# A pair's hash bits in one PSUM bank, their rows moved by DMA, and loads and transposes rearranged over the queues of a one-core attention and FFN kernel

## The chip, the cores and the metric

One core of one Trainium2 chip. The metric is device time in microseconds (us). Unless it says otherwise, a time is the median of a kernel's runs, and a line from a profile is from one profiled run of that kernel. A run is marked slow when it lies over 1.5% above the fastest of the same kernel; comparisons use the fast ones. Engine names: PE is TensorE's matmul, PEld its weight load, DVE VectorE, ACT ScalarE, POOL GpSimd, SP SyncE, whose queue here carries DMAs only. Two times belong to a DMA: its issue, in which the engine of its queue is held to hand it out, and its landing, from then until the data are there. The granted clock is the share of its full clock that TensorE was given (1.00 is full). In a line of a profile, `qT<-hb` reads "tile qT written from tile hb", and L205 is line 205 of that kernel.

## The reference, cut to what matters

```python
# q, k, v: (4 batches, 8 heads, 768 tokens, 64); proj: (64, 6)
q_bits = einsum('bhsd,dk->bhsk', q, proj) > 0          # six hash bits a token
k_bits = einsum('bhsd,dk->bhsk', k, proj) > 0
mask   = q_bucket[:, :, :, None] == k_bucket[:, :, None, :]
scores = where(mask, q @ k.T / 8, -1e9)
attn   = softmax(scores) @ v                           # then heads side by side: x is (3072, 512)
h      = maximum(maximum(x @ w1, x @ w2), x @ w3)      # three times 512 -> 768
out    = h @ w_out                                     # 768 -> 512
```

## The kernel before

Heads are worked in pairs, four pairs a batch. q and k are split into an fp16 high part and an fp16 residual, transposed, and multiplied by the two halves of `proj` (PA and PB, 32 columns each, so four groups lie side by side in a PSUM bank). The sign of each bit, scaled, becomes rows 64 to 69 of the transposed q and k. The scores then contract over 70 rows, and a pair in different buckets gets so low a score that its exponential is zero. So the first score of a pair waits for: load, splits, transpose, hash matmuls, compare, rows.

The program is a list of 192 steps, 48 a batch. A step is one score unit (two matmuls and one exponential) and whatever preparation the schedule puts there with `at(step, fn)`; FFN matmuls ("atoms") fill in as a credit allows. They share three PSUM buffers with the transposes and hash matmuls.

```python
def xbar(n, b, pr):                       # transpose by DMA, on SP's queue
    nc.sync.dma_start_transpose(T[n, b, pr][:], S16[n, b, pr][:].rearrange("p a d -> p (a d)"))

def hash_half(b, pr, half):               # one PSUM bank and one compare for each half of the tokens
    ...
    hps = hash_mm([(tq, 0, half), (tk, 0, half), (tq, 1, half), (tk, 1, half)])
    hash_cmp(hbs[b, pr][:, half * HQ : (half + 1) * HQ], hps)

def hash_rows(b, pr, heads=(0, 1)):       # DVE copies 6 partitions at a time, scaling them
    ...
        dst = T[n, b, pr][D : D + NBITS, hh * NCH : (hh + 1) * NCH, :].rearrange("p a t -> p (a t)")
        hash_row(dst, hb[32 * g : 32 * g + NBITS, :])

def prep(b, pr, s, lead, lag):            # pairs of batches 1 to 3
    at(s - lead, lambda: load_pair(b, pr, nc.gpsimd))
    ...
        at(s + 2 * i, lambda n=n: split_h(n, b, pr, nc.vector))
        at(s + 2 * i + 1, lambda n=n: split_r(n, b, pr))
        at(s + 2 * i + 1, lambda n=n: xbar(n, b, pr))
    tail(b, pr, s + lag)                  # hash_half, hash_half, hash_rows, hash_rows, one a step
```

Within a step the order is: score, attend, the scheduled functions, FFN atoms.

The softmax here doesn't subtract the row's maximum and nothing guards it: scores larger than these inputs give would overflow.

## Time and profile before

| | before |
|---|---|
| median of 3 runs | 340.19 us (340.01, 340.19, 345.54; the last a slow one) |
| span of the profiled run | 336.0 us |
| first score | 11.2 us |
| first score to first FFN matmul (stage A) | 54.8 us |
| first FFN matmul to last score (stage B) | 246 us |
| last score to the end (stage C) | 24.0 us |

The three stages have different limits, so they are read apart: in A there is no FFN work yet to fill PE with, in B PE should never stand, C is the last FFN half behind the last score. The lines are in the prediction below. One is added here, stage B as a whole (columns: stretch, length, busy time of PE, PEld, DVE, ACT and POOL, then the clock granted to PE, the DMA share, GB/s):

```profile
66.00:312.00 246.00, 220.75 (x2163) 135.94 (x2160) 153.01 (x299) 151.88 (x200) 42.85 (x53) 0.94 0.56 101
```

PE is idle for 25 of these 246 us and runs at 0.94 of its clock. The lines that matter here of what it waited for in the whole run (engine, tile and line, what it waited for; total us, times, longest):

```profile
PE tps L161 <- DVE qs L151: 6.9, 2, 5.0
PE ps L311 <- DVE ht L318: 5.2, 4, 3.1
PE hps L176 <- DMA kT<-ks: 4.6, 3, 3.4
PE xps L297 <- DVE ht L318: 4.2, 2, 2.8
...
PE hps L176 <- DMA qT<-qs: 3.3, 1, 3.3
```

The first is mostly the start, before the first score (5.0 us). For the rest, PE waits for DVE's max (`ht`, which frees a PSUM buffer), 12.7 us with the smaller lines, and the hash matmuls wait for DMA transposes.

### The profile page before, as it was taken

What the parts mean: (1) busy time and instruction counts of PE and PEld (TensorE: products, weight loads), DVE (VectorE), ACT (ScalarE), POOL (GpSimd) and SP (SyncE); (2) the same over time, 40 slices, a digit from 0 to 9 for tenths busy, and PEclk for the clock granted to TensorE, in tenths of its full rate; (3) what the DMA queues carried; (4) which work ended last, traced back from release to release, by engine and by line L of the source; (5) the groups of instructions that cost most, each with busy time, mean ns of one, the idle gap of its engine ahead of it and who ended that gap; (6) DMA issues with size and microseconds to landing.
All of it is one profiled execution on the core that took longest, in us unless ns stands there. A gap on an engine that the chain in (4) does not pass through costs nothing.

```text
span 336.0 us, 6898 instructions
## 1 busy us (share of the span) xinstructions
PE 288.1 (86%) x2800; PEld 177.3 (53%) x2800; DVE 212.6 (63%) x424; ACT 195.0 (58%) x254; POOL 67.8 (20%) x89
## 2 busy tenths in 40 slices
PE   1798696966998969799698987969989999999795
PEld 1465474542565546366365654636655666665352
DVE  3688969652998585937549585593775544453452
ACT  2467657651766647377275762746756776777120
POOL 1225625441041130403104040040200000000000
PEclk9999878595999999989699995997999999999899
DMA  7909989999969693590903927069442001001002
GB/s 228 334 3 142 208 168 237 161 181 106 200 93 155 142 162 76 106 221 13 210 16 107 223 59 177 22 139 124 53 91 97 2 0 64 33 0 64 32 2 94
DMA packets 52481, 38.20 MB, mean 114 GB/s; under 512 B 39009, under 2 KB 46497, under 8 KB 52449
## 3 DMA queue, kind: packets, MB, share of 16 engines
q1 hardware_dynamic: 44240, 20.26, 33.7%
q0 software_dynamic: 7984, 17.30, 23.7%
q8 instruction: 22, 0.36, 0.4%
q10 hardware_dynamic: 224, 0.20, 0.3%
q14 instruction: 11, 0.08, 0.1%
HBM read 25.17 MB, written 6.29 MB: 94 GB/s over the span
## 4 chain that ended last, share of the span: by engine, by line
PE 56%; DVE 24%; DMA 15%; issue 3%; ACT 1%; ACTq 0%; SPq 0%; DVEq 0%
PE ps L311 23%; PE sc L246 13%; DMA kT<-ks 13%; PE av L266 7%; PE po L323 6%; DVE qs L151 4%; DVE kT L185 3%; DVE ks L145 3%; DVE qT L185 3%; PE hps L176 3%; DVE ks L151 3%; DVE hb L181 2%; DVE ht L318 2%; PE tps L161 2%; DMA k<-in_k_dram 1%
## 5 line engine op out<-in xcount | busy, mean ns | idle before, releaser
L250 ACT ACTIVATE AT<-sc,bias_t 128x768 f16<-128x768 f32 x192 | 170.4, 903 | 97.8 <-PE sc L246 96.9
L311 PE MATMUL ps<-xT,w_sb 128*128 128x384 f16 x576 | 118.6, 342 | 8.7 <-DVE ht L318 5.2
L246 PE MATMUL sc<-qT,kT 70*128 70x384 f16 x384 | 102.2, 349 | 2.2 <-DVE qT L185 1.2
L318 DVE TENSOR_TENSOR ht<-ht,ps 128x384 f16<-128x384 f16 x96 | 52.9, 551 | 52.0 <-PE ps L311 49.3
L266 PEld LDWEIGHTS <-AT 128*128 128x128 f16 x1152 | 64.4, 101 | 33.7 <-issue 10.5
L311 PEld LDWEIGHTS <-w_sb 128*128 128x128 f16 x576 | 53.1, 101 | 42.4 <-issue 18.1
L266 PE MATMUL av<-vone,AT 128*128 128x65 f16 x1152 | 70.2, 198 | 3.4 <-DVE t L282 2.7
L287 POOL TENSOR_TENSOR xn<-t,rr 128x384 f16<-128x384 f32 x24 | 20.9, 870 | 224.4 <-DVE rr L285 134.7
L246 PEld LDWEIGHTS <-kT 70*128 70x128 f16 x384 | 34.6, 103 | 26.0 <-issue 10.0
L316 ACT CAST ht<-ps 128x384 f16<-128x384 f32 x48 | 22.8, 476 | 25.2 <-PE ps L311 25.1
L323 PE MATMUL po<-wout_sb,ht 128*128 128x512 f16 x144 | 35.0, 380 | 2.6 <-DVE ht L318 2.5
L181 DVE TENSOR_SCALAR hb<-hps 128x384 f16<-128x384 f32 x32 | 17.4, 545 | 22.9 <-PE hps L176 22.9
L282 DVE TENSOR_TENSOR t<-av,mv 128x390 f32<-128x390 f32 x32 | 17.9, 560 | 10.9 <-PE av L266 10.8
L323 PEld LDWEIGHTS <-ht 128*128 128x128 f16 x144 | 12.9, 97 | 16.3 <-DVE ht L318 3.0
L151 DVE SCALAR_TENSOR_TENSOR qs<-q,qs 128x768 f16<-128x768 f32 (+1 forms) x17 | 19.4, 1142 | 2.0 <-ACT qs L143 1.7
L329 DVE COPY osb<-po 128x512 f32<-128x512 f32 x16 | 11.0, 690 | 12.1 <-PE po L323 12.0
L217 POOL CAST vone<-v 128x768 f16<-128x768 f32 x16 | 15.1, 941 | 14.8 <-DMA v<-in_v_dram 14.8
L151 DVE SCALAR_TENSOR_TENSOR ks<-k,ks 128x768 f16<-128x768 f32 (+1 forms) x17 | 15.9, 936 | 2.3 <-ACT ks L143 1.9
L297 PE MATMUL xps<-iden,xn 128*128 128x128 f16 x96 | 11.5, 233 | 6.8 <-DVE ht L318 4.2
L176 PE MATMUL hps<-kT,PA 128*32 128x384 f16 x64 | 12.6, 366 | 5.4 <-DMA kT<-ks 4.6
L298 DVE COPY xT<-xps 128x384 f16<-128x384 f16 x32 | 11.3, 352 | 8.3 <-PE xps L297 7.8
L176 PE MATMUL hps<-qT,PA 128*32 128x384 f16 x64 | 13.0, 365 | 4.1 <-DMA qT<-qs 3.3
(46 smaller groups left out, 190.8 us busy)
## 6 DMA issues: line engine op xcount, KB each, us to landing
out_dram<-osb SPq DMA_DIRECT2D x24, 256.0 KB, 2.3
q<-in_q_dram POOLq DMA_DIRECT2D x12, 384.0 KB, 3.8
k<-in_k_dram POOLq DMA_DIRECT2D x12, 384.0 KB, 5.9
v<-in_v_dram POOLq DMA_DIRECT2D x12, 384.0 KB, 9.5
w_sb<-in_moe_w_dram POOLq DMA_DIRECT2D x6, 384.0 KB, 6.1
v<-in_v_dram SPq DMA_DIRECT2D x4, 384.0 KB, 6.5
q<-in_q_dram SPq DMA_DIRECT2D x3, 384.0 KB, 6.3
k<-in_k_dram SPq DMA_DIRECT2D x3, 384.0 KB, 6.8
```

The source lines that it names most:

```text
L151: nc.vector.scalar_tensor_tensor(out=s[:, a, D : 2 * D], in0=x32, scalar=QS, in1=s[:, a, 0:D], op0=AluOp.mult, op1=AluOp.subtract)
L176: nc.tensor.matmul(hps[32 * g : 32 * (g + 1), 0:HQ], w[:], t[:, a : a + CH, :], start=s, stop=not s)
L181: nc.vector.tensor_scalar(out=out, in0=hps[:, 0:HQ], scalar1=0.0, scalar2=0.5, op0=AluOp.is_gt, op1=AluOp.subtract)
L185: nc.vector.tensor_scalar(out=dst, in0=src, scalar1=2 * BIT, scalar2=None, op0=AluOp.mult)
L246: nc.tensor.matmul(sc[:, i, 0:HQ], kT[0:KR, hh * NCH + 2 * j + i, :], qT[0:KR, hh * NCH + hf * CH : hh * NCH + (hf + 1) * CH, :], start=Tr ...
L250: nc.scalar.activation(AT[:], sc[:, :, 0:HQ], ActFn.Exp, bias=bias_t[:], scale=EXP_SCALE)
L266: nc.tensor.matmul(av[:, o : o + D + 1], AT[:, i, c * P : (c + 1) * P], vones[b % 2][:, 2 * pr + hh, 2 * j + i, 0 : D + 1], start=first, s ...
L287: eng.tensor_tensor(out=xv, in0=t[:, :, :, 0:D], in1=rr[:].to_broadcast([P, 2, CH, D]), op=AluOp.mult)
L311: nc.tensor.matmul(ps[:, 0:HQ], w_sb[i][:, jc, fb * P : (fb + 1) * P], xT[:, jc, :], start=jc == 0, stop=jc == NJ - 1)
L316: nc.scalar.copy(ht[:], ps[:, 0:HQ])
L318: nc.vector.tensor_tensor(out=hts[fb][:], in0=hts[fb][:], in1=ps[:, 0:HQ], op=AluOp.max)
L323: nc.tensor.matmul(ps[:], hts[fb][:, c * P : (c + 1) * P], wout_sb[:, fb, :], start=fb == 0, stop=fb == NF - 1)
```

## The change

The intent: take work from DVE (the hash rows, half of the compares, the scaling half of the k splits), keep what is left of it out of the FFN's way, take batch 1's transposes from the DMA engines to PE, and keep Pool for the weights and for casting V.

```diff
-    raw = ... bufs=3        spl = ... bufs=2
+    raw = ... bufs=4        spl = ... bufs=3
-    load("k", 0, 0, nc.scalar, (0, 1))
+    load("k", 0, 0, nc.sync, (0, 1))
...
+    def hash_pair(b, pr):                       # both halves accumulate in one bank, 12 of 32 rows used
+        hb = small.tile([P, HQ], FP16, tag="hb", name="hb")
+        g = [(T[n, b, pr], hh) for hh in range(2) for n in "qk"]
+        hash_cmp(hb[:], hash_mm([[(t, hh, half) for t, hh in g] for half in range(2)]))
+        hash_row(hb[:], hb[:])                  # one scaling of the whole tile
+
+    def hash_rows(b, pr):                       # eight DMAs of 6 partitions x 768 bytes
+        ...
+                nc.sync.dma_start(T[n, b, pr][D : D + NBITS, a : a + CH, :].rearrange("p a t -> p (a t)"),
+                                  hb[o : o + NBITS, :])
...
     def front(b, pr, s):                        # TensorE transposes: batch 0, and now batch 1 too
+        at_end(s, lambda: split_h("q", b, pr, nc.vector))
+        at_end(s, lambda: split_h("k", b, pr, nc.vector if b == 0 else nc.scalar))
+        at_end(s, lambda: split_r("q", b, pr))
+        at_end(s + 1, lambda: split_r("k", b, pr))
...
     def prep(b, pr, s):                         # batches 2 and 3
+        at_end(s, lambda: split_h("q", b, pr, nc.vector))
+        at_end(s + 1, lambda: split_h("k", b, pr, nc.scalar))
+        at_end(s + 1, lambda: split_r("q", b, pr))
+        at_end(s + 1, lambda: xbar("q", b, pr))
+        at_end(s + 3, lambda: split_r("k", b, pr))
+        at_end(s + 3, lambda: xbar("k", b, pr))
+        tail(b, pr, s + 12)                     # hash_pair and hash_rows in one step
...
-                prep(b, pr, 26 + 7 * pr, 7, 12)
-                prep(b, pr, 2 * (b - 1) * NUG + 6 + 12 * pr, 10, 12)
+            s = 33 + 7 * pr if b == 1 else 2 * (b - 1) * NUG + 4 + 11 * pr
+            at(s - 8, lambda b=b, pr=pr: load_pair(b, pr, nc.sync))
+            (front if b == 1 else prep)(b, pr, s)
...
         if late:
             attend(u - LAG)
+        for fn in todo_end.pop(u, []):          # at_end: behind the step's FFN atoms
+            fn()
```

Cut: two sets of PA and PB (one for each half of the tokens), the copy of the first kT out of PSUM by DVE instead of ACT, PA and PB made behind the first splits, and smaller moves of the weight loads.

More of the change, by code (lines that the diff above doesn't have):

```diff
@@ L50 @@
     konst = ctx.enter_context(tc.tile_pool(name="konst", bufs=1))
-    raw = ctx.enter_context(tc.tile_pool(name="raw", bufs=3))
-    spl = ctx.enter_context(tc.tile_pool(name="spl", bufs=2))
+    raw = ctx.enter_context(tc.tile_pool(name="raw", bufs=4))
+    spl = ctx.enter_context(tc.tile_pool(name="spl", bufs=3))
     opnd = ctx.enter_context(tc.tile_pool(name="opnd", bufs=8))
@@ L104, with make_p @@
     ph = konst.tile([D, NBITS], FP16, name="ph")
-    PA = konst.tile([P, 32], FP16, name="PA")
-    PB = konst.tile([P, 32], FP16, name="PB")
-    nc.vector.memset(PA[:], 0.0)
-    nc.vector.memset(PB[:], 0.0)
     pr32 = konst.tile([D, NBITS], FP32, name="pr32")
-    def make_p():
-        nc.vector.tensor_copy(ph[:], p32[:])
-        nc.vector.tensor_tensor(out=pr32[:], in0=p32[:], in1=ph[:], op=AluOp.subtract)
+    PA, PB = [], []
+    for i in range(2):
+        for n, l in (("PA", PA), ("PB", PB)):
+            l.append(konst.tile([P, 32], FP16, name=f"{n}{i}", tag=f"{n}{i}"))
+            nc.vector.memset(l[i][:], 0.0)
+    def make_p(i):
+        if i == 0:
+            nc.vector.tensor_copy(ph[:], p32[:])
+            nc.vector.tensor_tensor(out=pr32[:], in0=p32[:], in1=ph[:], op=AluOp.subtract)
         for o in (0, D):
-            nc.vector.tensor_scalar(out=PA[o : o + D, 0:NBITS], in0=ph[:], scalar1=1024.0, scalar2=None,
-                                    op0=AluOp.mult)
-            nc.vector.tensor_scalar(out=PB[o : o + D, 0:NBITS], in0=pr32[:], scalar1=1024.0, scalar2=None,
-                                    op0=AluOp.mult)
+            for l, src in ((PA, ph), (PB, pr32)):
+                nc.vector.tensor_scalar(out=l[i][o : o + D, NBITS * i : NBITS * (i + 1)], in0=src[:],
+                                        scalar1=1024.0, scalar2=None, op0=AluOp.mult)
     w_sb = [konst.tile([P, NJ, DF], FP16, name=f"w{i}_sb") for i in range(3)]
@@ L169, in evac_T, with hash_mm @@
             nc.vector.tensor_copy(o, p16[:, c0 * P : c1 * P])
-    def hash_mm(groups):
+    def hash_mm(sets):
         hps = mm_ps.tile([P, 512], FP32, tag="mm", name="hps")
-        for s, w in ((True, PA), (False, PB)):
-            for g, (t, hh, half) in enumerate(groups):
+        ws = [(i, l[i]) for l in (PA, PB) for i in range(len(sets))]
+        for m, (i, w) in enumerate(ws):
+            for g, (t, hh, half) in enumerate(sets[i]):
                 a = hh * NCH + half * CH
                 nc.tensor.matmul(hps[32 * g : 32 * (g + 1), 0:HQ], w[:], t[:, a : a + CH, :],
-                                 start=s, stop=not s)
+                                 start=m == 0, stop=m == len(ws) - 1)
         return hps
@@ L187 @@
     hbs = {}
-    def hash_half(b, pr, half):
-        if half == 0:
-            hbs[b, pr] = small.tile([P, S], FP16, tag="hb", name="hb")
-        tq, tk = T["q", b, pr], T["k", b, pr]
-        hps = hash_mm([(tq, 0, half), (tk, 0, half), (tq, 1, half), (tk, 1, half)])
-        hash_cmp(hbs[b, pr][:, half * HQ : (half + 1) * HQ], hps)
-    def hash_rows(b, pr, heads=(0, 1)):
-        hb = hbs[b, pr]
-        for g, (n, hh) in enumerate((("q", 0), ("k", 0), ("q", 1), ("k", 1))):
-            if hh not in heads:
-                continue
-            dst = T[n, b, pr][D : D + NBITS, hh * NCH : (hh + 1) * NCH, :].rearrange("p a t -> p (a t)")
-            hash_row(dst, hb[32 * g : 32 * g + NBITS, :])
+    def hash_pair(b, pr):
+        hb = small.tile([P, HQ], FP16, tag="hb", name="hb")
+        hbs[b, pr] = hb
+        g = [(T[n, b, pr], hh) for hh in range(2) for n in "qk"]
+        hash_cmp(hb[:], hash_mm([[(t, hh, half) for t, hh in g] for half in range(2)]))
+        hash_row(hb[:], hb[:])
+    def hash_rows(b, pr):
+        hb = hbs.pop((b, pr))
+        for g, (n, hh) in enumerate((("q", 0), ("k", 0), ("q", 1), ("k", 1))):
+            for half in range(2):
+                a = hh * NCH + half * CH
+                o = 32 * g + NBITS * half
+                nc.sync.dma_start(T[n, b, pr][D : D + NBITS, a : a + CH, :].rearrange("p a t -> p (a t)"),
+                                  hb[o : o + NBITS, :])
     def hash_head(b, pr, hh):
         tq, tk = T["q", b, pr], T["k", b, pr]
-        hb = small.tile([P, S], FP16, tag="hb", name="hb")
-        hps = hash_mm([(tk, hh, 0), (tq, hh, 0), (tk, hh, 1), (tq, hh, 1)])
-        hash_cmp(hb[:, 0:HQ], hps)
+        hb = small.tile([P, HQ], FP16, tag="hb", name="hb")
+        hash_cmp(hb[:], hash_mm([[(tk, hh, 0), (tq, hh, 0), (tk, hh, 1), (tq, hh, 1)]]))
         for g, (t, half) in enumerate(((tk, 0), (tq, 0), (tk, 1), (tq, 1))):
@@ L212, in hash_head @@
             hash_row(t[D : D + NBITS, a : a + CH, :].rearrange("p a t -> p (a t)"),
-                     hb[32 * g : 32 * g + NBITS, 0:HQ])
+                     hb[32 * g : 32 * g + NBITS, :])
     def vcast(b, pr):
@@ L343, with at_end @@
     todo = {}
+    todo_end = {}
     def at(step, fn, pe=0.0):
         todo.setdefault(step, []).append((pe, fn))
+    def at_end(step, fn):
+        todo_end.setdefault(step, []).append(fn)
     operands(0, 0)
@@ L351 @@
     split_h("k", 0, 0, nc.scalar, (0, 1))
-    make_p()
     split_r("q", 0, 0, (0, 1))
     split_r("k", 0, 0, (0, 1))
+    make_p(0)
     pq = pe_T("q", 0, 0, 0)
@@ L357 @@
     evac_T(pq, "q", 0, 0, 0, nc.vector)
-    evac_T(pk, "k", 0, 0, 0, nc.scalar)
+    evac_T(pk, "k", 0, 0, 0, nc.vector)
     split_h("q", 0, 0, nc.scalar, (1, 2))
@@ L362 @@
     hash_head(0, 0, 0)
+    make_p(1)
     vcast(0, 0)
@@ L381, in front @@
         at(s, lambda: operands(b, pr))
-        at(s, lambda: split_h("q", b, pr, nc.vector))
-        at(s, lambda: split_r("q", b, pr))
-        at(s + 1, lambda: split_h("k", b, pr, nc.vector))
-        at(s + 1, lambda: split_r("k", b, pr))
+        at_end(s, lambda: split_h("q", b, pr, nc.vector))
+        at_end(s, lambda: split_h("k", b, pr, nc.vector if b == 0 else nc.scalar))
+        at_end(s, lambda: split_r("q", b, pr))
+        at_end(s + 1, lambda: split_r("k", b, pr))
         def tr(n, hh):
             evac_T(pe_T(n, b, pr, hh), n, b, pr, hh, nc.vector)
-        for i, (n, hh) in enumerate((("q", 0), ("k", 0), ("q", 1), ("k", 1))):
-            at(s + 3 + i // 2, lambda n=n, hh=hh: tr(n, hh), 0.34)
-        tail(b, pr, s + 5)
+        for i, (n, hh) in enumerate((("q", 0), ("q", 1), ("k", 0), ("k", 1))):
+            at(s + 2 + i // (2 if b == 0 else 1), lambda n=n, hh=hh: tr(n, hh), 0.34)
+        tail(b, pr, s + (4 if b == 0 else 7))
     def tail(b, pr, s):
-        at(s, lambda: hash_half(b, pr, 0), 0.34)
-        at(s + 1, lambda: hash_half(b, pr, 1), 0.34)
-        at(s + 2, lambda: hash_rows(b, pr, (0,)))
-        at(s + 3, lambda: hash_rows(b, pr, (1,)))
+        at(s, lambda: hash_pair(b, pr), 0.67)
+        at(s, lambda: hash_rows(b, pr))
     at(0, lambda: vcast(0, 1))
@@ L403 @@
     at(2, lambda: meanv(0, 0), 0.34)
-    at(5, lambda: load_pair(0, 3, nc.sync))
+    at(3, lambda: load_pair(0, 3, nc.sync))
     at(6, lambda: vcast(0, 2))
-    at(7, lambda: load_w(0, 0))
-    at(8, lambda: load_w(1, 0))
-    at(9, lambda: load_w(2, 0))
+    for i in range(3):
+        at(7 + i, lambda i=i: load_w(i, 0))
+        at(15 + i, lambda i=i: load_w(i, 1))
     front(0, 2, 11)
@@ L411, with prep @@
     at(15, lambda: vcast(0, 3))
-    front(0, 3, 19)
-    at(18, lambda: meanv(0, 2), 0.34)
-    for i in range(3):
-        at(16 + i, lambda i=i: load_w(i, 1))
+    front(0, 3, 18)
+    at(20, lambda: meanv(0, 2), 0.34)
     at(26, lambda: meanv(0, 3), 0.34)
-    at(20, lambda: nc.gpsimd.dma_start(wout_sb[:], moe_w_out.rearrange("(c p) m -> p c m", p=P)))
-    def prep(b, pr, s, lead, lag):
-        at(s - lead, lambda: load_pair(b, pr, nc.gpsimd))
+    at(18, lambda: nc.gpsimd.dma_start(wout_sb[:], moe_w_out.rearrange("(c p) m -> p c m", p=P)))
+    def prep(b, pr, s):
         at(s, lambda: operands(b, pr))
-        for i, n in enumerate("qk"):
-            at(s + 2 * i, lambda n=n: split_h(n, b, pr, nc.vector))
-            at(s + 2 * i + 1, lambda n=n: split_r(n, b, pr))
-            at(s + 2 * i + 1, lambda n=n: xbar(n, b, pr))
-        at(s + 4, lambda: vcast(b, pr))
-        tail(b, pr, s + lag)
-        at(s + lag + 4, lambda: meanv(b, pr), 0.34)
+        at_end(s, lambda: split_h("q", b, pr, nc.vector))
[5 more added lines that the diff above has]
+        tail(b, pr, s + 12)
     for b in range(1, B):
         for pr in range(NP):
-            if b == 1:
-                prep(b, pr, 26 + 7 * pr, 7, 12)
-            else:
-                prep(b, pr, 2 * (b - 1) * NUG + 6 + 12 * pr, 10, 12)
+            s = 33 + 7 * pr if b == 1 else 2 * (b - 1) * NUG + 4 + 11 * pr
+            at(s - 8, lambda b=b, pr=pr: load_pair(b, pr, nc.sync))
+            (front if b == 1 else prep)(b, pr, s)
+            at(s + 4, lambda b=b, pr=pr: vcast(b, pr))
+            at(s + 9, lambda b=b, pr=pr: meanv(b, pr), 0.34)
     N = len(units)
```

## The prediction

> **What bounds the kernel now.** I read the page first (busy shares, slices), then the chain of waits, then busy time by stretch, then the timeline around the holes.
>
> ```profile
> span 336.0 us, 6898 instructions
> PE 288.1 (86%) x2800; PEld 177.3 (53%) x2800; DVE 212.6 (63%) x424; ACT 195.0 (58%) x254; POOL 67.8 (20%) x89
> ...
> PEclk9999878595999999989699995997999999999899
> ...
> PE 56%; DVE 24%; DMA 15%; issue 3%; ACT 1%; ACTq 0%; SPq 0%; DVEq 0%
> ```
>
> PE has the most work, but 39% of the chain runs over DVE and DMA: PE waits for them, and the clock dips after such waits. I cut the span at the first score (11.2), the first FFN matmul (66), two points between, the last score (312) and the end. Columns: stretch, length, busy time of PE, PEld, DVE, ACT, POOL, then granted clock, DMA share, GB/s.
>
> ```profile
> 11.20:66.00 54.80, 46.77 (x522) 30.27 (x522) 45.27 (x88) 35.45 (x42) 23.24 (x29) 0.85 0.84 170
> 66.00:120.00 54.00, 44.84 (x452) 26.98 (x450) 36.62 (x74) 29.02 (x39) 13.52 (x17) 0.93 1.00 143
> 120.00:248.00 128.00, 111.93 (x1079) 68.67 (x1076) 85.47 (x161) 75.24 (x99) 24.34 (x31) 0.92 0.59 114
> 248.00:312.00 64.00, 63.98 (x638) 40.29 (x635) 30.91 (x65) 47.62 (x64) 4.99 (x6) 1.00 0.12 39
> 312.00:336.00 24.00, 18.09 (x99) 9.67 (x99) 9.72 (x19) 4.07 (x8) 0.00 (x0) 0.93 0.12 44
> ```
>
> The fourth stretch, with almost no preparation of later pairs in it, is the model: PE never idle, clock full, 48 score units in 64 us. Earlier stretches have holes. There are two kinds. Near 72 to 79 the hash matmuls wait for DMA transposes of batch 1; SP's transpose of kT took 12.79 us while loads shared the DMA engines:
>
> ```profile
> 61.07 12.79 SPq L155 DMA_TRANSPOSE kT<-ks  x1
> ...
> 75.46 0.34 PE L176 MATMUL hps<-qT,PA 128*32 128x384 f16 x1 [3.29 <-DMA qT<-qs]
> ...
> 79.15 0.48 PE L176 MATMUL hps<-kT,PA 128*32 128x384 f16 x1 [3.35 <-DMA kT<-ks]
> ```
>
> The other kind recurs once per prepared pair, about every 20 us from 120 to 246: DVE works through splits and hash rows, and the FFN's max, which frees PE's PSUM buffer, stands behind them in its queue.
>
> ```profile
> 157.21 1.43 DVE L151 SCALAR_TENSOR_TENSOR qs<-q,qs 128x768 f16<-128x768 f32 x1
> ...
> 159.14 0.40 DVE L185 TENSOR_SCALAR qT<-hb 6x768 f16<-6x768 f16 x1
> ...
> 159.57 0.57 DVE L185 TENSOR_SCALAR kT<-hb 6x768 f16<-6x768 f16 x1
> ...
> 160.17 1.06 DVE L145 TENSOR_SCALAR ks<-k 128x768 f16<-128x768 f32 x1
> 161.26 0.35 DVE L185 TENSOR_SCALAR qT<-hb 6x768 f16<-6x768 f16 x1
> 161.63 0.35 DVE L185 TENSOR_SCALAR kT<-hb 6x768 f16<-6x768 f16 x1
> 162.01 0.96 DVE L151 SCALAR_TENSOR_TENSOR ks<-k,ks 128x768 f16<-128x768 f32 x1
> 162.89 0.55 DVE L318 TENSOR_TENSOR ht<-ht,ps 128x384 f16<-128x384 f16 x1
> ...
> 163.49 1.44 PE L311 MATMUL ps<-xT,w_sb 128*128 128x384 f16 x4 [3.06 <-DVE ht L318]
> ```
>
> From 159.1 to 162.9 DVE does nothing for PE; PE stands 3.06 us, and its four matmuls then take 1.44 us where a warm group takes 0.81.
>
> **What the Trainium skill says.** (1) "TensorE: Matmul & The Clock Gate", Part 1: after an idle window of about 3.4 us the clock falls to half, and a similar busy window restores it. The trace agrees: after the 3.06 us hole the clock of 164 to 168 is 0.50. So each hole costs its length and then up to 2 us more. (2) "SBUF — State Buffer", Who interferes with whom: DVE and GpSimd share a port pair as an exclusive lock, and a DVE operation with two SBUF inputs collides with a GpSimd read. The trace agrees: the split that takes 0.96 us alone took 1.43 beside Pool's 0.83 us multiply at 157.00; the scaling of ks took 1.06 instead of 0.55 beside Pool's v cast at 159.96. (3) "TensorEngine Tiling (Array Packing)", Key Properties: a change of tiling mode drains TensorE. The trace is consistent: a warm group of eight 32-column hash matmuls, two rounds of four at 0.16, occupies 0.44 us. (4) "DMA: Bandwidth & Descriptors", Issuing engines are not separate DMA queues: all DMAs interleave on the same 16 engines. At the start k on ACT's queue took 4.94 us, issued at 1.33, against 2.5 for q issued at 0.74.
>
> **The change, part by part.**
>
> Start. k of head 0 follows q on one queue instead of being interleaved with everything. At 0.5 to 1 us after q (q is there at 3.26) it lands near 4 instead of 6.3. Less the kT evacuation moved to DVE and behind qT's (0.55), and make_p behind the splits, the first score moves from 11.2 to about 8.8.
>
> DVE. Hash rows: 60 of 6x768 go (14.4 + 13.8 = 28.2 us); 15 of 32 compares go (15 x 0.545 = 8.2); 12 ks scalings move to ACT (12 x 0.8 = 9.6); the lengthening of the splits beside Pool should mostly go with the Pool loads and the new order (15 x 0.26 = 4). Added: 15 scalings of hb, 128x384 f16 in SBUF, which I estimate at 0.2 us (PA's smallest cost 0.16, a 6x384 row 0.25), 3 us; 16 evacuations for batch 1's TensorE transposes, 16 x 0.55 = 8.8; 2 us of make_p and kT. Net 212.6 - 50 + 14 = about 177. More important, a pair's burst from qT rows to the k split (3.8 us) falls apart: nothing longer than one 0.96 split stands before a max, as splits now go at the end of a step.
>
> PE. 96 more transposes, in groups of 6 at 0.33 to 0.35: 16 x 0.34 = +5.4 us. Hash rounds are the same number (same matmuls), but 15 mode changes fewer at about 0.2 us: -3. Net +2.4, on the path.
>
> ACT. 12 k splits; 128x384 took 0.52, the exponential of 768 takes 0.90, so 0.9 each, +11 us on 195: 206 of some 300, not a bound except in the first stage.
>
> DMA. 8 of 24 transposes go. New: 15 pairs x 8 = 120 row DMAs of 4.5 KB. The 1.5 KB load of proj landed in 2.7 us and its issue took 0.55; eight issues at about 0.4 (SP's usual) and a landing make 5 to 6 us. The room from hash to first score is 6 steps for pair 1 and at least 5 for batch 1, at 1.2 to 1.5 us a step: 6 to 8 us. Hidden, narrowly. Pool loses 36 load issues of 0.73, 26 us.
>
> **The sum, by stage.** Stage A (first score to first FFN, 42 units, 54.8 us): the exponentials alone are 42 x 0.90 = 38; DVE, at 45.3 of 54.8, falls to some 35 (18 rows, 4 to 5 compares, and part of two batch-1 pairs' splits leave). So ACT bounds it; I allow 8 us of start-up and waits: 46. Ends at 8.8 + 46 = 55 instead of 66.
>
> Stage B (66 to 312, 151 units, 246 us): warm PE work from the trace's rates (four 384-column matmuls 0.65): 804 score and FFN matmuls x 0.1625 = 131; 126 of 512 columns x 0.217 = 27; 910 av x 0.03 = 27; hash 44 rounds x 0.1625 plus 22 x 0.2 = 12; xps and svp 147 x 0.055 = 8. Sum 205. The same sum for 248 to 312 gives 63 of its 64 us, so the accounting holds. The other 41 us of stage B: 26 idle (6.6 for transposes, 16 in DVE bursts, the rest small) and about 11 from half clock (clock deficit times length, by 4 us windows). After: 205 + 5 - 2 = 208, and I keep a quarter of the 41: 218.
>
> Stage C, the last FFN half behind the last score, is untouched: 24. Total 55 + 218 + 24 = 297 of span; runs lie 2 to 4 above the span (337.83 and 340.19 against 336): 300. I add 4 for waits I can't see: 304.
>
> **The rivals.** (a) SP as the new wait: its one in-order queue carries loads, transposes, rows and stores, and one blocked entry holds all behind it. SP was blocked 12.79 and 8.51 us by transposes while Pool loaded. For it: loads now precede each k transpose in the same queue. Against: loads lead by 8 steps (10 us), hash of batches 2 and 3 follows its transpose by 9 steps, and the longest transposes, batch 1's, are gone. If rows or loads come late in one pair out of three at 3 us each plus the clock, 315 to 325. (b) PE-bound anyway, holes only moved: PE's FFN quota is paced evenly by a credit, so a hole may reappear where ACT's k split (0.9) or the evacuations of batch 1 delay a max. For it: three PSUM buffers serve all of these. That keeps half of the 41: 315. (c) All better than thought, stage A at ACT's floor and stage B dense: 8.8 + 40 + 211 + 24 + 3 = 287. Getting slower would need (a) in nearly every pair.
>
> **Range and chances.** Centre 304; low 292 is close to (c), high 322 is (a) or (b) with a little more. Faster by over 2% means below 333.4, which wants only 7 of the 41 us back: 0.94; within 2% 0.05; slower 0.01.
>
> **What would show it.** Right: no PE hole over 1 us between first and last score, clock 1.0 through stages A and B after warm-up, first score near 9, first FFN matmul near 55, DVE busy near 177, no row copies on DVE. Wrong: PE's scores or score weights waiting for the row DMAs, splits waiting for loads of q or k, SP blocked for many microseconds ahead of rows, or ACT ending PE's waits.

## The result, and the profile after

The changed kernel takes **317.52 us** (316.73 to 318.67, four runs) against 340.1 of the kernel before in the same rounds. The ratio is 0.935, 95% interval 0.930 to 0.940: faster, inside the predicted range, but 13.5 us above the predicted 304. (A ratio is the mean time of one kernel's fast runs over that of the other's of the same rounds, so not quite the ratio of the medians.)

The page of the changed kernel, in the order of the prediction's first fence:

```profile
span 314.9 us, 7282 instructions
...
PE 279.7 (89%) x2896; PEld 180.2 (57%) x2896; DVE 178.7 (57%) x375; ACT 202.7 (64%) x265; POOL 41.3 (13%) x53
...
PEclk9999699999989997799999999999999999999999
...
PE 74%; DMA 12%; DVE 8%; ACT 3%; issue 2%; SPq 0%; ACTq 0%; DVEq 0%
```

DVE's share of the chain fell from 24% to 8%, as was meant; DMA's hardly moved, 15% to 12%. The clock row still has dips: the fifth slice (31.5 to 39.4 us) at 0.6, the twelfth at 0.8, and the 16th, 17th and 19th (118 to 150 us) at 0.7. The stages, cut at the first score, the first FFN matmul and the last score of this run:

```profile
8.70:63.90 55.20, 46.14 (x547) 32.34 (x547) 34.76 (x75) 36.12 (x43) 14.34 (x17) 0.94 0.74 175
63.90:292.00 228.10, 214.55 (x2232) 137.10 (x2229) 128.71 (x260) 159.20 (x210) 26.28 (x30) 0.98 0.39 101
292.00:314.90 22.90, 16.68 (x109) 9.27 (x105) 10.03 (x19) 4.36 (x8) 0.00 (x0) 0.97 0.12 46
```

| | before | predicted | after | after minus predicted |
|---|---|---|---|---|
| first score | 11.2 | 8.8 | 8.7 | -0.1 |
| stage A | 54.8 | 46 | 55.2 | +9.2 |
| stage B | 246 | 218 | 228.1 | +10.1 |
| stage C | 24.0 | 24 | 22.9 | -1.1 |
| run less span | 1.8 (337.83 - 336.0) | 3, and 4 for unseen waits | 1.8 (316.73 - 314.9) | -5.2 |

So the start and the end came out as predicted, stage A gained nothing at all, and stage B gained 18 where 28 was predicted. The longest of what PE waited for in the whole run (the second is again mostly the start, 4.2 us):

```profile
PE hps L179 <- DMA kT<-ks: 8.8, 4, 4.3
PE tps L162 <- DVE qs L152: 6.8, 5, 4.2
PE ps L314 <- DVE mv L231: 4.2, 2, 2.5
PE sc L249 <- DMA kT<-hb: 3.3, 2, 2.1
```

The waits for DVE's max are gone. In their place stand the k transposes (8.8 us instead of 4.6, although there are 8 instead of 12 of them) and a new wait for the row DMAs, `kT<-hb`. Both are entries of SP's queue. Stage A shows the rows of pair 1 (start, duration, engine, line, operation, tiles; in brackets the idle time before and what ended it):

```profile
24.68 1.63 SPq L205 DMA_DIRECT2D qT<-hb  x2
...
26.36 1.43 SPq L205 DMA_DIRECT2D kT<-hb  x2
...
27.84 1.61 SPq L205 DMA_DIRECT2D qT<-hb  x2
...
29.50 1.43 SPq L205 DMA_DIRECT2D kT<-hb  x2
29.63 0.50 PE L249 MATMUL sc<-qT,kT 70*128 70x384 f16 x2 [2.05 <-DMA kT<-hb]
...
31.86 0.50 PE L249 MATMUL sc<-qT,kT 70*128 70x384 f16 x1 [1.26 <-DMA kT<-hb]
```

Eight issues fill SP from 24.68 to 30.93, 6.2 us. PE stands 2.05 and 1.26 us for the rows, and the next stretch runs at half clock:

```profile
32.00:36.00 4.00, 4.00 (x39) 3.50 (x38) 2.38 (x6) 1.80 (x2) 2.39 (x4) 0.50 0.91 142
```

The rows of pairs 2 and 3 fill the queue again, from 39.0 to 44.9 and from 46.5 to 52.3 us, and only then, at 52.41, does SP issue the first load of batch 1, which the schedule had put at step 25. In stage B, the largest hole:

```profile
101.12 1.49 SPq L205 DMA_DIRECT2D qT<-hb  x2
...
107.51 0.95 DVE L152 SCALAR_TENSOR_TENSOR ks<-k,ks 128x768 f16<-128x768 f32 x1
...
111.59 1.43 SPq L205 DMA_DIRECT2D kT<-hb  x2
...
113.10 1.46 SPq L156 DMA_TRANSPOSE qT<-qs  x1
...
114.61 0.87 SPq L78 DMA_DIRECT2D q<-in_q_dram  x1
...
115.54 1.15 SPq L78 DMA_DIRECT2D k<-in_k_dram  x1
...
117.81 2.76 SPq L156 DMA_TRANSPOSE kT<-ks  x1
...
123.18 0.48 PE L179 MATMUL hps<-kT,PA 128*32 128x384 f16 x1 [4.30 <-DMA kT<-ks]
```

The split that the k transpose reads is done at 108.46. But the rows of two pairs, 16 issues, fill SP from 101.12 to 113.02, and behind them the k transpose stands after q's transpose, the next pair's loads of q, k and v and a store. It is issued at 117.81, and the PE work that needs it starts at 123.18. PE waits 4.30 us, and the clock of 124 to 128 is 0.50.

### The profile page after: what moved, and what is told of

Its sections match the earlier page's. It is cut to its first block, busy times and chain, and to the rows that moved or that the text cites. A ratio compares the mean times of both kernels' runs of the same rounds, so it can differ in the third digit from the quotient of the medians.

```text
span 314.9 us, 7282 instructions
## 1 busy us (share of the span) xinstructions
PE 279.7 (89%) x2896; PEld 180.2 (57%) x2896; DVE 178.7 (57%) x375; ACT 202.7 (64%) x265; POOL 41.3 (13%) x53
## 4 chain that ended last, share of the span: by engine, by line
PE 74%; DMA 12%; DVE 8%; ACT 3%; issue 2%; SPq 0%; ACTq 0%; DVEq 0%
PE ps L314 27%; PE sc L249 17%; PE po L326 9%; PE av L269 9%; DMA kT<-ks 7%; PE hps L179 5%; PE tps L162 4%; ACT AT L253 3%; DMA k<-in_k_dram 2%; PE xps L300 2%; DVE ks L152 2%; DMA kT<-hb 1%; PE svp L228 1%; DMA q<-in_q_dram 1%; DVE hb L184 1%
## 5 line engine op out<-in xcount | busy, mean ns | idle before, releaser
L314 PE MATMUL ps<-xT,w_sb 128*128 128x384 f16 x576 | 112.8, 330 | 4.2 <-DVE mv L231 4.2
L249 PE MATMUL sc<-qT,kT 70*128 70x384 f16 x384 | 98.6, 339 | 7.0 <-DMA kT<-hb 3.3
L269 PEld LDWEIGHTS <-AT 128*128 128x128 f16 x1152 | 62.4, 99 | 28.9 <-issue 4.6
L269 PE MATMUL av<-vone,AT 128*128 128x65 f16 x1152 | 68.4, 196 | 1.4 <-ACT AT L253 0.7
L314 PEld LDWEIGHTS <-w_sb 128*128 128x128 f16 x576 | 51.3, 98 | 31.7 <-issue 6.4
L184 DVE TENSOR_SCALAR hb<-hps 128x384 f16<-128x384 f32 x17 | 9.5, 557 | 20.9 <-PE hps L179 20.8
L179 PE MATMUL hps<-kT,PA 128*32 128x384 f16 x64 | 9.6, 363 | 9.7 <-DMA kT<-ks 8.8
L152 DVE SCALAR_TENSOR_TENSOR qs<-q,qs 128x768 f16<-128x768 f32 (+1 forms) x17 | 15.4, 906 | 0.2
L162 PE MATMUL tps<-iden,qs 128*128 128x128 f16 x96 | 9.4, 254 | 6.8 <-DVE qs L152 6.8
L144 ACT ACTIVATE ks<-k 128x768 f16<-128x768 f32 (+1 forms) x14 | 11.1, 796 | 4.0 <-DMA k<-in_k_dram 4.0
```

The lines of the kernel that those rows point to most:

```text
L152: nc.vector.scalar_tensor_tensor(out=s[:, a, D : 2 * D], in0=x32, scalar=QS, in1=s[:, a, 0:D], op0=AluOp.mult, op1=AluOp.subtract)
L162: nc.tensor.transpose(p16[:, c * P : (c + 1) * P], S16[n, b, pr][:, hh * NCH + c, :], iden[:])
L179: nc.tensor.matmul(hps[32 * g : 32 * (g + 1), 0:HQ], w[:], t[:, a : a + CH, :], start=m == 0, stop=m == len(ws) - 1)
L249: nc.tensor.matmul(sc[:, i, 0:HQ], kT[0:KR, hh * NCH + 2 * j + i, :], qT[0:KR, hh * NCH + hf * CH : hh * NCH + (hf + 1) * CH, :], start=Tr ...
L269: nc.tensor.matmul(av[:, o : o + D + 1], AT[:, i, c * P : (c + 1) * P], vones[b % 2][:, 2 * pr + hh, 2 * j + i, 0 : D + 1], start=first, s ...
L314: nc.tensor.matmul(ps[:, 0:HQ], w_sb[i][:, jc, fb * P : (fb + 1) * P], xT[:, jc, :], start=jc == 0, stop=jc == NJ - 1)
```

## The experiments

My theory: SP's queue is the new bound on both waits, because one row DMA occupies SP for longer than predicted. Rivals: the rows are late because of their landing, not their issue; the schedule puts transposes too late behind the loads; batch 1's TensorE transposes or the k split on ACT cost what DVE gained. All outputs are right. All edits are to the changed kernel. A table of times stands at the end of this section.

**1. Shorter issues, as many of them.** Copy 16 partitions instead of 6; the ten extra land in rows of the transposed tile that no score reads.

```diff
-   nc.sync.dma_start(T[n, b, pr][D : D + NBITS, ...], hb[o : o + NBITS, :])
+   nc.sync.dma_start(T[n, b, pr][D : D + 16, ...],    hb[o : o + 16, :])
```

> The changed kernel with each row DMA widened from 6 to 16 partitions (the ten extra rows of qT and kT are no longer read). Theory I, SP's issue time per row DMA is what was mis-sized (0.66 to 0.72 us, loads over 128 partitions take 0.41): if the issue time is tied to the odd partition count it falls to about 0.4, eight rows take 3.5 instead of 5.8 us, holes shrink, and the time falls by 4 to 8 us to 310 to 314. If the issue stays at 0.66, no change within 1%. Rival II, the holes are the engines' landing time behind loads and transposes: no change, or slightly slower for 2.7 times the row bytes.

The issues of one tile in the changed kernel (count, then ns least/median/most):

```profile
L205 SPq DMA_DIRECT2D kT<-hb x60: 658/662/677, 26.4 to 236.2; - x60
```

and with 16 partitions:

```profile
L205 SPq DMA_DIRECT2D kT<-hb x60: 507/553/1566, 23.7 to 230.9; - x60
```

More data, shorter issue, and 314.63 us instead of 317.52. The size of the copy isn't what costs; the time on the queue is a candidate. By itself the gain is not clear: the fast runs, 312.31 to 316.46, come near those of the changed kernel (316.73 and up), and the intervals of the two ratios overlap (0.916 to 0.935 and 0.930 to 0.940).

**2. Half as many.** Hash in two banks as before (two compares, two scalings), and one row DMA of 6 x 1536 bytes for each tensor and head: four a pair.

```diff
+   for half in range(2):
+       o = hb[:, half * HQ : (half + 1) * HQ]
+       hash_cmp(o, hash_mm([[(t, hh, half) for t, hh in g]]))
+       hash_row(o, o)
...
-   for half in range(2): ...                  # eight DMAs of 6 x 768 bytes
+   dst = T[n, b, pr][D : D + NBITS, hh * NCH : (hh + 1) * NCH, :].rearrange("p a t -> p (a t)")
+   nc.sync.dma_start(dst, hb[32 * g : 32 * g + NBITS, :])
```

> The changed kernel with the hash in two banks and two compares again, but four row DMAs of 6 x 1536 B a pair in place of eight. Theory I: SP spends 2.8 instead of 5.8 us a pair; the hole of 3.3 us near 28 us and most of those in front of hash matmuls near 119, 193 and 211 shrink; DVE gets 15 x 0.8 = 12 us and PE some 3 us more work; 308 to 314. Rival II (landing, not issue): no better than 317, rather 319 for the added work.

305.07 us (the three fast runs 304.77 to 305.33; the profiled run was a slow one at 329.91 with a clock of 0.846 and isn't used), ratio 0.897 to the kernel before. 12 us come back although DVE does 15 compares and 15 scalings more. One issue still takes 0.67.

**3. As many, on two queues.** q's rows on SP, k's rows on Pool.

```diff
+   eng = nc.sync if n == "q" else nc.gpsimd
-   nc.sync.dma_start(T[n, b, pr][...], hb[...])
+   eng.dma_start(T[n, b, pr][...], hb[...])
```

> The changed kernel with the four k rows issued by Pool and the four q rows by SP. Theory I: the two queues issue side by side, rows complete about 3 us earlier and SP has 2.9 us a pair more for loads and transposes: 309 to 314. Against it: Pool's issues take 0.73 each, and Pool also multiplies xn and casts v, so x transposes may come later. Rival II: no change.

```profile
L206 SPq DMA_DIRECT2D qT<-hb x60: 659/667/1002, 23.4 to 222.2; - x60
L206 POOL DMA_DIRECT2D kT<-hb x60: 518/521/709, 24.0 to 222.0; - x60
```

The wait for k transposes, and the one wait for rows that is left:

```profile
PE hps L179 <- DMA kT<-ks: 0.7, 1, 0.7
...
51.70 0.68 PE L250 MATMUL sc<-qT,kT 70*128 70x384 f16 x2 [2.84 <-DMA kT<-hb]
```

306.66 us, ratio 0.902. This run decides between number and queue: the same eight DMAs of the same size, with nothing else changed, are as good as four. It also ties both waits to one cause: the wait for k transposes falls from 8.8 us to 0.7, though no transpose was moved, because SP reaches it sooner: it issues the transpose of the hole above at 112.83 instead of 117.81. The wait that is left is for pair 3's rows. Their issues end at 46.98 on Pool and 47.55 on SP, so what remains until 51.70 is, as far as the profile shows, landing beside batch 1's loads, which begin at 47.63. The rival of late landing is thus not nil, but it is this one hole. Stage A gains nothing here (54.9 us); the whole gain is stage B, 217.2 us instead of 228.1.

**4. No row DMA at all.** The hash halves and DVE rows of the kernel before, in the changed kernel's schedule.

```diff
-   at(s, lambda: hash_pair(b, pr), 0.67)
-   at(s, lambda: hash_rows(b, pr))
+   at(s, lambda: hash_half(b, pr, 0), 0.34)
+   at(s + 1, lambda: hash_half(b, pr, 1), 0.34)
+   at(s + 2, lambda: hash_rows(b, pr, (0,)))
+   at(s + 3, lambda: hash_rows(b, pr, (1,)))
```

> The changed kernel with the hash rows written by DVE as before (two banks, two compares, four 6x768 row copies, no row DMA); all else of the change stays. Theory I: SP free, so no wait for rows, transposes or loads, but DVE gains some 33 us and its bursts come back in front of the max: 310 to 320. Rival III, the gain of the change came mainly from taking the rows off DVE: 325 or more.

312.91 us, ratio 0.922, DVE busy 207.5 us instead of 178.7. So the row DMAs as the change has them lose to the DVE copies, with their two banks, that they replace (317.5 against 312.9), and four of them beat both (305.1). It also says where the change's gain comes from: the 28 us from 340.8 to 312.9 come from the rest of it, and the rows as moved take some of them back. And no wait for k transposes is left here, though the loads still stand ahead of them in SP's queue: it took the rows to make them late.

**5. Both cures.** Four row DMAs of 16 partitions.

```diff
-   nc.sync.dma_start(T[n, b, pr][D : D + NBITS, ...], hb[32 * g : 32 * g + NBITS, :])   # experiment 2
+   nc.sync.dma_start(T[n, b, pr][D : D + 16, ...],    hb[32 * g : 32 * g + 16, :])
```

> Both cures at once: four row DMAs a pair, each over 16 partitions. Theory I: SP's row time falls from 4 x 0.71 to 4 x 0.55, and since four DMAs already left no hole behind rows or transposes, little is left to win: 302 to 306. If issue time still bounded something: below 301.

304.25 us (300.09 to 305.54), one issue 0.54 us. Its fast runs are 300.09 and 303.24, those of the same four DMAs without the widening 304.77 to 305.33 (experiment 2) and 300.92 and 303.69 (experiment 9): not told apart. The kernel before had one run at 331.48 that made its others count as slow, so there is no ratio for this and the next three.

**6. Loads back on Pool.**

```diff
-   at(s - 8, lambda b=b, pr=pr: load_pair(b, pr, nc.sync))
+   at(s - 8, lambda b=b, pr=pr: load_pair(b, pr, nc.gpsimd))
```

> The changed kernel with the q/k/v loads of batches 1 to 3 issued by Pool again. SP then has only rows, transposes and stores. If SP's queue is the wait (theory I), rows no longer delay loads and loads no longer delay k transposes, so the holes near 56, 119, 193 and 211 shrink and the time falls to 308 to 314, against which DVE pays 3 to 4 us for collisions with Pool. If what matters of the change is loads off Pool (the collisions), it rises to 321 or more.

328.44 us; the three fast runs 326.91 to 328.44, the profiled run a slow one. I had expected 308 to 314, and that reading fell: emptying SP of loads costs 10 us. In one place a transpose meets loads that Pool issues:

```profile
198.25 0.72 POOL L78 DMA_DIRECT2D v<-in_v_dram  x1
...
200.27 6.23 SPq L156 DMA_TRANSPOSE kT<-ks  x1
...
209.48 0.50 PE L179 MATMUL hps<-qT,PA 128*32 128x384 f16 x1 [4.97 <-DMA qT<-qs]
```

A k transpose's issue, 1.59 to 3.13 us in the changed kernel, holds SP for 6.23 beside Pool's loads, as the 12.79 us of the kernel before did, and the wait for q's transpose there is 4.97 us. The other seven k transposes take 1.30 to 3.52, so this is one hole and not a rule. The waits for rows rose too, from 3.3 to 6.6 us. DVE's busy time is 179.4, as in the changed kernel: longer DVE instructions don't explain the 10 us. What does, beyond these holes, is not shown.

**7. Batch 1 by DMA transposes again**, at the kernel before's steps.

```diff
-   s = 33 + 7 * pr if b == 1 else ...
-   (front if b == 1 else prep)(b, pr, s)
+   s = 26 + 7 * pr if b == 1 else ...
+   prep(b, pr, s)
```

> The changed kernel with batch 1 prepared by DMA transposes again, with the lead of the kernel before (steps 26 + 7 pr), all loads on SP. My prediction held the TensorE transposes to be worth 6.6 us of holes and some 5 of half clock less 5.4 us of PE work, so 5 to 8: expected 322 to 330 here, with holes at hash matmuls between 55 and 110. Rival: the slow transposes of before came from Pool's loads alone, and behind loads in one queue they are quick: 313 to 318, PE 5 us less busy.

323.7 us: 6 us slower. The wait of hash matmuls for k transposes rises from 8.8 to 15.2 us, six times, up to 5.0. Moving batch 1 to PE is worth its 5 us of PE time in this schedule. Not all of the 6 us are transposes: with the earlier steps ACT comes to batch 1's k split before its load is there, and PE stands 4.30 us at 54.10 behind ACT.

**8. The k split on DVE.**

```diff
-   split_h("k", b, pr, nc.scalar)
+   split_h("k", b, pr, nc.vector)
```

> The changed kernel with the 12 scalings of ks for batches 1 to 3 on DVE again, at the same places in the order. DVE +7 to 10 us, ACT -10. As these stand at the end of a step and DVE has room, I expect 316 to 320, no change within 1%. If the k split on ACT held up the exponentials: 313 or less. If DVE's load matters as much as I argued for the bursts: 321 or more.

320.21 us (317.62 to 322.91) against 317.52, in different rounds: within 1%, so the k split on ACT neither costs nor gives much.

**9. Four row DMAs, run again** beside the next two, with the edit of experiment 2.

> The four-row-DMA kernel once more, for a profile in the fast state: 305 us, first FFN matmul near 58, no PE wait above 0.5 us for a row DMA and none above 1 us for a transpose.

305.08 us (300.92 to 307.0), the same as in experiment 2. The profile I expected nearly came: the first FFN matmul at 59.6, no wait for rows above 0.2 us, but one of 1.2 for a k transpose. Stage A is 50.4 us in it and stage B 219.7; it is a run marked slow, with a clock of 0.989. In this group the kernel before spread from 334.77 to 349.74, so the verdict on all three kernels was unclear in form; their slowest run, 307.0, is still 27 us below its fastest.

**10. Four wide row DMAs, and batch 0's splits in the order in which PE needs them** (q high, q residual, k high; without the second set of PA and PB, which two banks don't need).

```diff
-   make_p(1)
     at_end(s, lambda: split_h("q", b, pr, nc.vector))
-    at_end(s, lambda: split_h("k", b, pr, ...))
     at_end(s, lambda: split_r("q", b, pr))
+    at_end(s, lambda: split_h("k", b, pr, ...))
```

> Four wide row DMAs, and in batch 0 the q split is finished before the k split begins, and the second pair of projection weights (not needed with one set a bank) is left out. If the 0.7 to 1.1 us hole near 17 us is what keeps PE's clock at half until 23 us in the changed kernel (18.6 in the kernel before), the clock rises about 3 us sooner and the first stage ends 2 to 4 us earlier: 299 to 302. If the hole doesn't matter (its place in the clock's window does): 303 to 305.

302.57 us (297.88, 301.58, 303.56, 304.3). One or two us below experiment 5, which the spread does not settle. Its profile shows the run that the prediction had described:

```profile
8.70:56.40 47.70, 40.50 (x547) 28.02 (x547) 36.43 (x78) 35.66 (x43) 13.69 (x16) 1.00 0.86 205
56.40:273.30 216.90, 210.25 (x2233) 134.94 (x2230) 137.00 (x283) 158.96 (x211) 26.44 (x30) 1.00 0.41 109
273.30:295.90 22.60, 16.67 (x108) 9.26 (x104) 10.01 (x19) 4.35 (x8) 0.00 (x0) 0.99 0.12 46
```

Stage A 47.7, B 216.9, C 22.6 at full clock, where 46, 218 and 24 were predicted. This is the fastest of its four runs, so it is the best case, not the usual one.

**11. The same with batches 2 and 3 four steps later**, to move the hole that waits for `mv`.

```diff
-   s = ... 2 * (b - 1) * NUG + 4 + 11 * pr
+   s = ... 2 * (b - 1) * NUG + 8 + 11 * pr
```

> The same, with the preparation of batches 2 and 3 four steps later, so that pair 0 of batch 2 no longer splits its k in the same step as pair 3 of batch 1: the hole of 2.5 us near 88 us (PE waiting for mv behind two k splits beside Pool's casts) and the half clock after it go: 3 to 4 us faster than the run before it, 296 to 299. If those holes only move: the same within 1 us.

302.8 us (301.72 to 303.83). The hole at 2.53 us shrank to 1.03, and others of 1.12 and 2.83 us appeared near 99 us (for rows) and 201 us (for a k transpose): nothing gained.

**12. Splits and transposes back at their place early in a step**, rows untouched (eight on SP).

```diff
     def at_end(step, fn):
-        todo_end.setdefault(step, []).append(fn)
+        todo.setdefault(step, []).append((0.0, fn))
```

> The changed kernel with splits and DMA transposes placed early in their step, as before the change, instead of at its end. I predicted that taking the splits out from in front of the FFN's max was a main part of the 16 us won in DVE bursts. If so, holes in front of PE that wait for a max or an output copy come back, 1 to 2 us for each of the 12 pairs of batches 1 to 3 at worst: 322 to 330. Rival: the burst was broken by taking the rows and the k scaling off DVE, and the place in the step doesn't matter: 316 to 320.

309.49 us (fast runs 304.3 and 308.8; 310.18 and 312.28 marked slow), ratio 0.900 (0.882 to 0.918; the verdict unclear in form again). I had expected 322 to 330, the rival 316 to 320: both fell, on the same side. The trace of a slow run, at clock 0.960, shows why:

```profile
117.66 2.73 SPq L156 DMA_TRANSPOSE kT<-ks  x1
...
120.44 0.58 SPq L78 DMA_DIRECT2D q<-in_q_dram  x1
...
122.25 0.32 PE L179 MATMUL hps<-kT,PA 128*32 128x384 f16 x1 [0.51 <-DMA kT<-ks]
```

The k transpose now precedes the next pair's loads in SP's queue, and all waits for k transposes together are 0.5 us instead of 8.8. (Compare the order and not the times: this run is 3 us later here, with a hash compare shortly before at 103.01 instead of 100.00.) The burst of DVE work that `at_end` was to break up came back only in small part: PE waits four times for the max, 4.2 us in all and 2.2 at the longest, against 12.7 us in the kernel before. So the end-of-step placement, the part meant to help the FFN, cost the changed kernel about 8 us (317.5 against 309.5, in different rounds), and the trace puts it to the order that it gave SP's queue. With experiment 4 this makes the late k transposes the work of two things together, rows and loads ahead of them: taking either away ends the wait. Stage A, where pair 1's rows still come late, stays long in this run (8.7 to 65.9).

| kernel | median us | row issues a pair on SP: number x us | ratio of fast runs |
|---|---|---|---|
| the changed kernel | 317.52 | 8 x 0.66 = 5.3 | 0.935 |
| 1, 16 partitions | 314.63 | 8 x 0.55 = 4.4 | 0.926 |
| 3, k's rows on Pool | 306.66 | 4 x 0.67 = 2.7 | 0.902 |
| 2 and 9, four row DMAs | 305.07, 305.08 | 4 x 0.67 = 2.7 | 0.897, 0.894 |
| 5, four wide ones | 304.25 | 4 x 0.54 = 2.2 | none |
| 10, four wide ones, order of splits | 302.57 | 4 x 0.54 = 2.2 | 0.896 |
| 11, and batches 2, 3 later | 302.8 | 4 x 0.54 = 2.2 | 0.895 |
| 12, splits early, eight rows | 309.49 | 8 x 0.66 = 5.3 | 0.900 |
| 4, rows on DVE | 312.91 | none | 0.922 |
| 8, k split on DVE | 320.21 | 8 x 0.66 | none |
| 7, batch 1 by DMA transposes | 323.7 | 8 x 0.66 | none |
| 6, loads on Pool | 328.44 | 8 x 0.66 | none |

Over the first five rows, where only the row DMAs and what feeds them differ, time falls with SP's time for them and not with their number or size; the last three of the five lie within each other's spread. The version to keep is four row DMAs a pair (2, 5 or 10): about 302 to 305 us, faster than both kernels. Experiments 2 and 12 together were not run.

## Why the prediction was right or wrong

The direction and the range held. The centre was 13.5 us too low, and one step, the DMA step, made most of that. The range held because its upper part was put there for rival (a), which is near to what happened; the main line's own mechanism, rows that are hidden, did not hold.

**The start: right.** First score at 8.70 for 8.8; k of head 0 was there at 3.71 for "near 4".

**DVE: right in total.** 178.7 us for 177. Within it, the scaling of hb took 0.26 us for 0.2. The lengthened splits only half went: the mean q residual split fell from 1.22 to 0.95 us, but that of k rose from 0.99 to 1.06, beside Pool's cast of v. Experiment 4 puts 28.8 us back on DVE: 24.4 of row copies (28.2 in the kernel before) and 8.1 of compares, less 4.1 of scalings. One reading in point (2) does not fit the rule that it is put under: the slow scaling of ks, 1.06 us for 0.55, reads one tile and not two.

**ACT: right.** 202.7 us for 206, and experiment 8 finds nothing to gain by taking the k split off it.

**PE: nearly right.** The saving of a pair's hash matmuls in one bank instead of two is about 0.1 us (0.77 us against twice 0.44), where 0.2 was put down (the prediction's own line, 0.44 against two rounds of 0.16, gives 0.12); that is 1.5 us over 15 pairs. Busy time in the dense run of experiment 10, which hashes in two banks again, is 210 us in stage B for the predicted 208.

**The DMA step: wrong, and it is the step that failed.** The prediction said "eight issues at about 0.4 (SP's usual) and a landing make 5 to 6 us" and "Hidden, narrowly". The 0.4 was the issue of a 128-partition load; a row of 6 partitions holds SP for 0.66 to 0.67 us, and with the steps between them two take 1.48 us from start to start. So the eight issues alone take about 5.9 us, not 3.2, before the last landing; in a kernel whose rows are 24 KB, the landing is 1.8 us. The room of 6 to 8 us is used up, and what stands behind the rows in the same queue is late as well: pair 1's scores, batch 1's loads, and each k transpose. Its main line asked only whether the rows arrive in time for their own scores, not what 15 x 5.9 = 88 us of SP's queue would do to the other entries. Experiments 2 and 3 show this; 1 and 5 fit it, but their gains lie within the spread.

**The sums by stage.** Stage A stayed at 55.2 instead of 46, and B took 228.1 instead of 218. Stage B came to 217.2 with k's rows on Pool and to 219.7 with four row DMAs: the 208 plus a quarter of the lost 41 us was sound once SP was freed. Stage A was not: with four row DMAs it took 50.4 us, and with no row DMA at all (experiment 4) 52.0, so the rows explain some 5 of its 9 us. It came to 47.7 only in the best run of experiment 10, and what the last 4 us are is open. The run lay 1.8 us above its span, not 3, and the 4 us for waits that I could not see were too few.

**"Nothing longer than one 0.96 split stands before a max": right in effect, wrong in its price.** The max waits are gone, but experiment 12 shows that they stay small (4.2 us) without the end-of-step placement, and that this placement puts the k transposes behind the next pair's loads. The prediction's rival (a) named the mechanism: "one blocked entry holds all behind it" and "loads now precede each k transpose in the same queue". I argued against it with the lead of the loads and the 9 steps' room, which holds for a queue that is otherwise empty. Its size was right in stage B (waits of 4.3, 2.3 and 2.0 us), while its 315 to 325 is where the result lies.

**Pool.** I gave the move of loads to SP only 26 us of Pool's time. Experiment 6 shows another worth: with the loads back on Pool the kernel is 10 us slower. That loads then meet transposes is seen in one hole of 5 us; as the cause of all 10 it is not shown.

**Open.** The two waits for `mv`, 4.2 us in all, stand in most versions; they are 2.8 in experiment 11, 1.1 in 12, and gone in 7, where batch 1 has DMA transposes. I take them for splits ahead of `mv` on DVE beside Pool's cast: in experiment 10 two k splits take 2.94 us there, beside two casts, where one alone takes 0.95. No run isolated that. Nor is it settled how much of experiment 10's best run is the order of the splits and how much is a PE clock that was full earlier, since the same kernel also ran at 304.3.

## What to carry to other kernels

When copies move from a compute engine to DMAs, count what each one occupies of the queue that issues it, number times issue time, and ask what stands behind them there; an engine that "does no work" can be full. Fewer DMAs, or the same ones over two queues, were worth 11 to 12 us here, while the data moved didn't matter. On an in-order queue also put what is needed next ahead of what is needed later: transposes behind rows and a prefetch cost 8.8 us of waits here.

## What the Trainium skill lacked or had wrong

- "DMA: Bandwidth & Descriptors", Issuing engines are not separate DMA queues: it calls the time to initiate a DMA "usually small relative to the DMA itself". Here one row's issue took 0.66 us and its landing 1.7 to 1.8 (on Pool, and for 24 KB on SP), so a pair's eight issues, 5.9 us, outlast a landing, and spreading the issues over two queues took the kernel from 317.5 to 306.7 us. It has no issue time by shape (only one figure per instruction for earlier chips, in its part on trn3): 0.66 to 0.67 us for 6 partitions on SP, 0.54 to 0.55 for 16, about 0.41 for a load of 128 partitions, 0.52 for 6 partitions on Pool.
- No page that I read says what loads from another queue do to a DMA transpose: the issue of a k transpose took 1.59 and 1.74 us with no load just ahead in SP's queue and 1.99 to 3.13 behind loads there (changed kernel), and up to 6.23 and 12.79 us beside Pool's loads.
- "TensorE: Matmul & The Clock Gate", Part 1, tells of an idle window of some 3.4 us. Here shorter holes were followed by half clock: one of 3.06 us in the kernel before, which the prediction's point (1) took as agreement, and two of 2.05 and 1.26 us with about 1 us of work between them (0.50 from 32 to 36 us). A hole of 2.53 us was followed by half rate in the changed kernel (four FFN matmuls 1.44 us, at 91.99) and by full rate in experiment 10 (0.81 us, at 85.65). And the granted clock reads 1.00 at 8.70 us while two score matmuls take 0.80 us, against 0.49 at 24.06: early in the run the durations tell more than that column.
